# Attention with a top-32 mask and a gated layer: from one slot at a time to pairs of slots, with scores, two sets of values and scores side by side

## The chip, the cores and the metric

The kernel runs on one core of a Trainium2 chip. The metric is the device time of one execution in microseconds. The core has a matmul engine (TensorE, PE in the profile), a vector engine (VectorE, DVE), an engine for functions of one element (ScalarE, ACT), a general one (GpSimd, POOL) and a queue that issues all DMAs here (SyncE, SP). Each takes its own instructions in the order in which the program lists them; semaphores order them among each other.

## The reference

Eight batches, eight heads, 576 positions, 64 elements per head; all in float32.

```python
scores = scale * np.matmul(q, k.transpose(0, 1, 3, 2))       # scale = 1/8
kth = np.partition(scores, -32, axis=-1)[..., -32:-31]
scores = np.where(scores >= kth, scores, -1000000000.0)
scores = scores - np.max(scores, axis=-1, keepdims=True)
attn = np.exp(scores)
attn = attn / (np.sum(attn, axis=-1, keepdims=True) + 1e-09)
attn_out = np.matmul(attn, v)
x = attn_out.transpose(0, 2, 1, 3).reshape(4608, 512)
h = x @ w_in                                                 # 512 -> 2048
out = (h * (1.0 / (1.0 + np.exp(-1.702 * h)))) @ w_out       # 2048 -> 512
```

## The kernel before, in words

**Slots.** The work on attention is cut into 144 slots, 18 per batch. A full slot is one tile of 128 query rows of two heads (four row tiles by four head pairs, 16 slots). The 64 rows that are left over (576 is 4.5 x 128) make two ends slots per batch, each with four heads. In an even batch the ends slots come last, in an odd batch first, so that four ends slots stand together: slots 16 to 19, 52 to 55, 88 to 91, 124 to 127.

**Steps of a slot.**
- `prepare` (L185): TensorE transposes a loaded q or k of two heads in four 128x128 blocks into one PSUM bank; ScalarE copies it to `q_t` or `k_t` (L195). With a k, the 64 leftover rows of q and k are transposed too (L199), into a second bank, and copied out (L200, L202).
- `scores` (L215): matmuls over 64 rows, with the two heads on the two halves of the array (shape 64*128, at ends slots 64*64), into `s_ps`, two tiles of two banks each. ScalarE copies them to `sc` (L232), which has three buffers.
- `topk` (L234): on VectorE, eight largest at a time for each head (L241), then their removal (L244); 14 operations. `two_slots` calls it within `find`.
- `bounds` (L255), two small operations on GpSimd, and `exponentials` (L263), four operations on ScalarE with their sums, writing `pr`.
- `divide` (L276): VectorE takes the reciprocal of the sums; from slot 9 on ScalarE scales the first head's half of `pr` (L288) and GpSimd the second's (L289).
- `turn_main` and `turn_ends` (L312, L316): TensorE transposes `pr` into `tp`; ScalarE copies it to `pt` (L310).
- `values` (L322): TensorE multiplies `pt` with v. The two heads use the two column halves (shape 128*64). ScalarE copies to `xT` (L344, L349).
- `hidden` (L364): 512 hidden units for a tile of 128 tokens, 32 matmul instructions into the only bank of `ph`. `tanh` (L385) has ScalarE make the tanh of it and a copy `h`, and `gate` (L397) multiplies them on GpSimd (in the first ten slots and at the end on VectorE, straight from `ph`). `project` (L411) adds the result's share of the output in `po`, eight matmul instructions. A token tile takes four rounds of these; there is one round per slot.

**PSUM.** `s_ps` takes four banks, `ph` one, `po` one. The other two are the ring `tp`, from which `prepare`, `turn` and `values` take a bank in turn.

**Weights.** The two weight matrices come in 32 pieces during the first nine slots (two to four per slot, `by_slot`). `round_piece` (L122) takes each through five steps: `size` (ScalarE), `shift` (VectorE, L143), `low` and `sign` (ScalarE), `finish` (two GpSimd operations, L138 and L139, in the following slot). The shifts stand between the operations of `topk`, after the seventh.

**Order.** The order of instructions is written out by hand: `slot(n)` lists them. It begins with the loads that the table `later` holds for this slot, then bounds and exponentials of slot n-1, preparations and scores of slot n+2 (up to slot 6), sizes, tanh, the top-k of slot n with the division of n-1 after its sixth operation, and the gate. From slot 7 on ("settled") come preparations, projection, turning and values of n-1, the scores of n+2 and the hidden round:

```python
        if settled and n + 2 < N:
            scores(n + 2)
        hidden()
```

Three tables give the slot, counted from the first slot of a batch, in which a head pair's q and k are loaded (`FETCH`) and prepared (`READY`), and its v loaded (`VALUES`).

Of the kernel before, what the change touches and what calls it, by code (L numbers as in the profile page):

```python
# [9 lines left out]
ALU = mybir.AluOpType  # L10
ENG = mybir.EngineType
F32 = mybir.dt.float32
U32 = mybir.dt.uint32
# [3 lines left out]
P = 128  # L17
# [11 lines left out]
def kernel(  # L29
# [24 lines left out]
    nc = tc.nc  # L54
# [11 lines left out]
    G = 4  # L66
    NG = FC // G
    PIECE = 512
# [8 lines left out]
    SETTLED = 9  # L77
# [3 lines left out]
    const = ctx.enter_context(tc.tile_pool(name="const", bufs=1))  # L81
# [20 lines left out]

    ident = const.tile([P, P], F32, name="ident")
    make_identity(nc, ident[:])
    win = const.tile([P, CC, DFF], F32, name="win")
    wout = const.tile([P, FC, C], F32, name="wout")

# [14 lines left out]
    def round_piece(n):  # L122

        c, g = pieces[n]
        dst = wout[:, g, :] if c is None else win[:, c, g * PIECE : (g + 1) * PIECE]
        words = raw.pop(n)[:].rearrange("p (n w) -> p n w", w=2)
        low, high = words[:, :, 0], words[:, :, 1].bitcast(F32)
        bits, whole = dst.bitcast(U32), dst.bitcast(I32)

        def finish():
            nc.gpsimd.tensor_tensor(out=whole, in0=whole, in1=low.bitcast(I32), op=ALU.add)  # L138
            nc.gpsimd.tensor_tensor(out=dst, in0=dst, in1=high, op=ALU.mult)  # L139

        return {
            "size": lambda: nc.scalar.activation(dst, high, AF.Abs, scale=REBASE),
            "shift": lambda: nc.vector.tensor_scalar(bits, bits, 3, None, op0=ALU.logical_shift_left),  # L143
            "sign": lambda: nc.scalar.activation(high, high, AF.Sign),
            "low": lambda: nc.scalar.mul(out=low.bitcast(I32), in_=low, mul=2.0**-29),
            "finish": finish,
        }
# [37 lines left out]
    def prepare(name, b, hp):  # L185
        src = loaded.pop((name, b, hp))


        before = 0 if name == "q" else TAIL
        dst = qkt.tile([P, S + before], F32, name=f"{name}_t")  # L190
        full = ps_t.tile([P, 512], F32, name="tp")
        for t in range(NF):
            nc.tensor.transpose(full[:, t * P : (t + 1) * P], src[:, t, :, :], ident[:])  # L193
        scale = SCALE if name == "q" else 1.0
        nc.scalar.mul(out=dst[:, before : before + FULL], in_=full[:], mul=scale)  # L195
        (qT if name == "q" else kT)[b, hp] = dst
        if name == "k":
            ends = ps_t.tile([P, 512], F32, name="tp")
            nc.tensor.transpose(ends[:, 0:P], loaded.pop(("ends", b, hp))[:], ident[:])  # L199
            nc.scalar.mul(out=qT[b, hp][:, FULL:S], in_=ends[:, 0:TAIL], mul=SCALE)  # L200
            for to in (0, before + FULL):
                nc.scalar.copy(out=dst[:, to : to + TAIL], in_=ends[:, TAIL:P])  # L202
# [8 lines left out]
    N = len(slots)  # L211
    PER = N // B
    st = [{} for _ in slots]

    def scores(n):  # L215
        b, t, hps = slots[n]
        ps = [ps_s.tile([P, 2, 512], F32, name="s_ps") for _ in range(2)]
        if t < NF:
            parts = [(i, 0, slice(0, P), slice(t * P, (t + 1) * P)) for i in range(2)]
        else:  # L220
            parts = [(i, p, slice(p * TAIL, (p + 1) * TAIL), slice(FULL, S)) for i, p in ((0, 0), (1, 1), (0, 1), (1, 0))]
        for c in range(2):
            for i, p, rows, cols in parts:
                on = slice(i * D, (i + 1) * D)
                nc.tensor.matmul(  # L225
                    ps[i][rows, c, 0:HALF],
                    lhsT=qT[b, hps[p]][on, cols],
                    rhs=kT[b, hps[p]][on, FIRST[i] + c * HALF : FIRST[i] + (c + 1) * HALF],
                )
        sc = st[n]["sc"] = scp.tile([P, 2, S], F32, name="sc")  # L230
        for i in range(2):
            nc.scalar.copy(out=sc[:, i, :].rearrange("p (c k) -> p c k", c=2), in_=ps[i][:, :, 0:HALF])  # L232
# [22 lines left out]
    def bounds(n):  # L255

        top = st[n]["top"]
        cut = st[n]["cut"] = small.tile([P, 2], F32, name="cut")
        low = st[n]["low"] = small.tile([P, 2], F32, name="low")
        nc.gpsimd.tensor_scalar(cut[:], top[:, :, TOPK - 1], -1.0, None, op0=ALU.mult)  # L260
        nc.gpsimd.tensor_tensor(out=low[:], in0=top[:, :, TOPK - 1], in1=top[:, :, 0], op=ALU.subtract)
# [50 lines left out]
    def turn_main(n):  # L312
        for i in range(2):
            turn(n, i * NF, MAIN[i], NF)

    def turn_ends(n):  # L316

        turn(n, 2 * NF, FULL, 1)
# [42 lines left out]
    to_gate, gated, to_project = [], [], []  # L361
    proj = {}

    def hidden():  # L364
        if not ready:
            return
        xT, rows = ready[0]
        g = hidden_at["g"]
        ph = ps_h.tile([P, G, P], F32, name="ph")
        for i in range(G):  # L370
            f = g * G + i
            for c in range(CC):
                nc.tensor.matmul(  # L373
                    ph[:, i, :],
                    lhsT=win[:, c, f * P : (f + 1) * P],
                    rhs=xT[:, c, :],
                    start=(c == 0),
                    stop=(c == CC - 1),
                )
        to_gate.append((ph, g, rows))  # L380
        hidden_at["g"] = (g + 1) % NG
        if g == NG - 1:
            ready.pop(0)
# [47 lines left out]
    later = {}  # L431
# [4 lines left out]

    READY = (((-9, -8), (-7, -6), (-5, -4), (-3, -2)), ((-7, -6), (-5, -4), (-3, -3), (-2, -2)))
    FETCH = (((-13, -12), (-11, -10), (-7, -6), (-5, -4)), ((-11, -10), (-9, -8), (-6, -5), (-4, -3)))  # L440
    VALUES = ((-8, -7, -1, 0), (-8, -7, 0, 0))
    by_slot = dict(enumerate([2, 3, 4, 4, 4, 4, 3, 4, 4]))
    for n in by_slot:
        first = sum(map(len, list(by_slot.values())[:n]))
# [19 lines left out]
    def slot(n):  # L464
        todo = later.pop(n, [])
        for fn, args in todo:
            if fn is not prepare:
                fn(*args)
        preparing = [args for fn, args in todo if fn is prepare]
        settled = n > PROJECTS  # L470
        aside = SETTLED < n < N
        before = 0 <= n - 1 < N
        if before:
            bounds(n - 1)
            exponentials(n - 1)
        if n < 0:
            for m in range(2):
                for args in preparing:
                    if args[2] == m:
                        prepare(*args)  # L480
                scores(m)
        elif not settled:
            for args in preparing:
                prepare(*args)
            scores(n + 2)
        some = [round_piece(x) for x in by_slot.get(n, [])]
        for piece in some:
            piece["size"]()
        shifts = [piece["shift"] for piece in some]
        tanh(aside)  # L490
        for i, op in enumerate(topk(n) if 0 <= n < N else [lambda: None] * 14):
            op()
            if i == 2 and unfinished:
                unfinished.pop(0)()
            if i == 5:
                if before:
                    divide(n - 1)
                while unfinished:
                    unfinished.pop(0)()
            if i == 11 and not aside:  # L500
                gate(aside)
            if i > 6 and shifts:
                shifts.pop(0)()
        if aside:
            gate(aside)
        if settled:
            for args in preparing:
                prepare(*args)
        for piece in some[:2]:
            piece["low"]()  # L510
        going = settled and len(to_project) > (2 if n < N else 0)
        if going:
            project(range(G - 1))
        if before:
            turn_main(n - 1)
        if going:
            project(range(G - 1, G))
        if before:
            turn_ends(n - 1)
        for piece in some[2:]:  # L520
            piece["low"]()
        if before:
            values(n - 1)
        for piece in some:
            piece["sign"]()
            unfinished.append(piece["finish"])
        if settled and n + 2 < N:
            scores(n + 2)
        hidden()

    with tc.manual_schedule():
        for n in range(-1, N + 1):
            slot(n)
        n = N + 1
        while ready or to_gate or gated or to_project:
            slot(n)
            n += 1
# [30 lines left out]
```

## Time and profile before

| | |
|---|---|
| median of 3 runs | 1668.62 us (1666.99 to 1668.85) |
| span of the profiled execution | 1667.9 us |
| busy: PE, DVE, ACT, POOL | 96%, 88%, 69%, 45% |
| slots 0 to 8 (with weight steps), start to start on DVE | 19.0 us, then 13.6 to 14.9 us |
| settled full slots without preparation | 10.60 us |
| settled full slots with a q, with a k | 11.04, 11.15 us |
| slots 16, 17, 52, 53, 88, 89, 124, 125 | 13.43 us six times, 13.71 and 15.13 us |
| last top-k operation to the end | 47 us |

A slot is read on VectorE from its first L241 on `sc` to the next slot's. In the chain of waits each line gives a start, a length and the work that the end depended on at that time; lengths there are from start to the next start, so that they add up. A matmul's modelled duration in the timeline is longer than its step, since matmuls overlap. A float32 matmul of two operand tiles appears as two instructions. The shape after MATMUL (128*128, 64*128, 128*64) gives the rows and columns of the array that one instruction uses.

### The profile page before, as it was taken

How to read it: one execution, taken by the hardware profiler on the slowest of the kernel's cores; microseconds unless marked ns; L12 is line 12 of the kernel's file. 1: busy time of each engine (PE TensorE's matmuls, PEld its weight loads, DVE VectorE, ACT ScalarE, POOL GpSimd, SP SyncE). 2: the span in 40 equal slices, each digit the busy share in tenths (PEclk: the TensorE clock that was granted, in tenths of full speed). 3: DMA queues.
4: the chain of work that ended last, by engine and by line, in shares of the span. 5: the costliest groups of instructions: out<-in, count | busy, mean ns of one | idle time of the engine just before them, and what ended most of it. 6: DMA issues, size and time to landing. Idle time of an engine off the chain costs nothing.

```text
span 1667.9 us, 31998 instructions
## 1 busy us (share of the span) xinstructions
PE 1599.2 (96%) x11923; PEld 1174.2 (70%) x11923; DVE 1468.8 (88%) x3210; ACT 1155.7 (69%) x2450; POOL 753.0 (45%) x785
## 2 busy tenths in 40 slices
PE   5579999999999999999999999999999999999999
PEld 3466767777777767777777776777777776777776
DVE  4999989998999988998899997999899998899980
ACT  5987766677766676667776676667777676777661
POOL 1787434444444443444444443444444444444440
PEclk7789999999999999999999999999999999999999
DMA  7342100110001100111001110011000110000000
GB/s 211 115 151 62 23 23 14 36 36 22 21 8 42 29 22 22 36 28 30 22 7 28 29 36 16 8 36 36 22 21 8 43 29 22 22 7 8 7 8 13
DMA packets 125723, 56.59 MB, mean 34 GB/s; under 512 B 116864, under 2 KB 116864, under 8 KB 125568
## 3 DMA queue, kind: packets, MB, share of 16 engines
q1 hardware_dynamic: 125568, 54.55, 12.4%
q8 instruction: 94, 1.54, 0.4%
q14 instruction: 61, 0.50, 0.1%
HBM read 45.09 MB, written 9.44 MB: 33 GB/s over the span
## 4 chain that ended last, share of the span: by engine, by line
PE 87%; DVE 5%; ACT 5%; SPq 1%; issue 1%; POOL 1%; DMA 0%; POOLq 0%; ACTq 0%
PE ph L373 29%; PE po L421 29%; PE o L332 10%; PE s_ps L225 10%; PE tp L300 8%; DVE top L241 2%; DVE left L244 2%; ACT pr L271 1%; PE tp L193 1%; ACT sc L232 1%; DVE wout L143 1%; ACT sc L269 1%; ACT pr L288 0%; SPq L160 0%; DVE win L143 0%
## 5 line engine op out<-in xcount | busy, mean ns | idle before, releaser
L241 DVE MAX8 top<-left 128x8 f32<-128x576 f32 x864 | 610.0, 746 | 0.0
L289 POOL TENSOR_SCALAR pr<-pr,rden 128x576 f32<-128x576 f32 x135 | 232.9, 1725 | 688.8 <-ACT th L390 640.7
L421 PE MATMUL po<-wout,gT 128*128 128x512 f32 x1152 | 542.4, 594 | 0.0
L373 PEld LDWEIGHTS ph<-xT,win 128*128 128x128 f32 x4096 | 470.6, 193 | 56.0 <-issue 47.6
L373 PE MATMUL ph<-xT,win 128*128 128x128 f32 x4096 | 494.4, 279 | 6.4 <-DVE gT L406 6.4
L244 DVE MATCH_REPLACE8 left<-top,left 128x576 f32<-128x576 f32 x576 | 423.3, 742 | 0.0
L310 ACT COPY pt<-tp 128x512 f32<-128x512 f32 (+1 forms) x432 | 193.4, 481 | 192.0 <-PE tp L300 185.6
L421 PEld LDWEIGHTS po<-wout,gT 128*128 128x128 f32 x1152 | 198.3, 192 | 142.6 <-issue 142.4
L232 ACT COPY sc<-s_ps 128x576 f32<-128x576 f32 x288 | 169.9, 642 | 134.8 <-PE s_ps L225 134.6
L271 ACT ACTIVATE pr<-sc,low 128x576 f32<-128x576 f32 x288 | 219.5, 767 | 0.0
L300 PEld LDWEIGHTS tp<-ident,pr 128*128 128x128 f32 x1215 | 145.0, 140 | 104.7 <-issue 42.3
L269 ACT ACTIVATE sc<-sc,cut 128x576 f32<-128x576 f32 x288 | 208.7, 779 | 9.2 <-POOL cut L260 9.2
L244 DVE MATCH_REPLACE8 left<-top,sc 128x576 f32<-128x576 f32 x288 | 211.6, 742 | 0.0
L241 DVE MAX8 top<-sc 128x8 f32<-128x576 f32 x288 | 201.9, 742 | 10.7 <-ACT sc L232 10.7
L403 POOL TENSOR_SCALAR th<-th 128x512 f32<-128x512 f32 x134 | 200.6, 1497 | 0.0
L225 PE MATMUL s_ps<-k_t,q_t 64*128 64x288 f32 (+1 forms) x1280 | 182.2, 431 | 1.3 <-ACT k_t L195 1.3
L300 PE MATMUL tp<-ident,pr 128*128 128x128 f32 x1215 | 177.2, 273 | 0.3 <-POOL pr L289 0.2
L404 POOL TENSOR_TENSOR gT<-th,h 128x512 f32<-128x512 f32 x134 | 171.5, 1280 | 11.2
L332 PEld LDWEIGHTS o<-pt,v_l 128*64 128x64 f32 x2560 | 128.0, 138 | 67.8 <-ACT pt L310 67.8
L332 PE MATMUL o<-pt,v_l 128*64 128x128 f32 (+1 forms) x2560 | 161.7, 269 | 0.2
L280 DVE TENSOR_SCALAR some<-den 128x2 f32<-128x2 f32 x144 | 24.1, 168 | 130.6 <-ACT pr L271 130.4
L225 PEld LDWEIGHTS s_ps<-k_t,q_t 64*128 64x128 f32 (+1 forms) x1280 | 99.6, 177 | 40.2 <-issue 20.9
(50 smaller groups left out, 1152.3 us busy)
## 6 DMA issues: line engine op xcount, KB each, us to landing
q_l<-in_q_dram SPq DMA_DIRECT2D x64, 128.0 KB, 2.5
k_l<-in_k_dram SPq DMA_DIRECT2D x64, 128.0 KB, 2.6
v_l<-in_v_dram SPq DMA_DIRECT2D x64, 128.0 KB, 2.5
raw<-in_moe_w_in_dram SPq DMA_DIRECT2D x16, 512.0 KB, 4.3
raw<-in_moe_w_out_dram SPq DMA_DIRECT2D x16, 512.0 KB, 3.7
out_dram<-ob SPq DMA_DIRECT2D x32, 256.0 KB, 2.1
ends<-in_q_dram SPq DMA_DIRECT2D x32, 32.0 KB, 2.3
ends<-in_k_dram SPq DMA_DIRECT2D x32, 32.0 KB, 2.4
```

The costliest lines, as they stand in the source:

```text
L225: nc.tensor.matmul(ps[i][rows, c, 0:HALF], lhsT=qT[b, hps[p]][on, cols], rhs=kT[b, hps[p]][on, FIRST[i] + c * HALF : FIRST[i] + (c + 1) * ...
L241: nc.vector.max(top[:, i, 8 * r : 8 * r + 8], (left if r else sc)[:, i, :])
L244: nc.vector.match_replace(left[:, i, :], top[:, i, 8 * r : 8 * r + 8], (left if r else sc)[:, i, :], LOWEST)
L269: nc.scalar.activation(sc[:, i, :], sc[:, i, :], AF.Prelu, bias=cut[:, i : i + 1], alpha=HUGE)
L271: nc.scalar.activation(pr[:, i * S : (i + 1) * S], sc[:, i, :], AF.Exp, bias=low[:, i : i + 1], accum_out=den[:, i : i + 1],)
L289: nc.gpsimd.tensor_scalar(pr[:, S : 2 * S], pr[:, S : 2 * S], rden[:, 1:2], None, op0=ALU.mult)
L300: nc.tensor.transpose(tp[:, c * P : (c + 1) * P], pr[:, at], ident[:])
L310: nc.scalar.copy(out=to, in_=tp[:, 0 : blocks * P])
L332: nc.tensor.matmul(o[j * D : (j + 1) * D, 0 : cols.stop - cols.start], lhsT=main[:, c, j, :] if c < NF else tail[:, j, :], rhs=pt[:, j * N ...
L373: nc.tensor.matmul(ph[:, i, :], lhsT=win[:, c, f * P : (f + 1) * P], rhs=xT[:, c, :], start=(c == 0), stop=(c == CC - 1),)
L403: nc.gpsimd.tensor_scalar(th[:], th[:], 1.0, None, op0=ALU.add)
L421: nc.tensor.matmul(po[:], lhsT=gT[:, i, :], rhs=wout[:, f, :], start=(f == 0), stop=(f == FC - 1))
```

## The change

Five things change.

1. From slot 10 on, `two_slots(n)` replaces two calls of `slot`. It softens n-1 (bounds and exponentials), finds the top-k of n, turns n-2, makes a hidden round, softens n, turns n-1, finds the top-k of n+1, and then has the scores of n+2, the values of n-2 and n-1, and the scores of n+3 in a row, with a second hidden round last. Values come one slot later relative to the rest than before. Up to four preparations have places: after the first gate, after the second gate, before the scores, and after the last scores.
2. `READY`, `FETCH` and `VALUES` have new entries for the later head pairs of a batch.
3. A piece's `shift` is a `scalar_tensor_tensor` with a second input, a column of zeros that is broadcast, in place of a `tensor_scalar`.
4. In the first slots all `size` steps come ahead of preparations and scores, and the gate on VectorE comes after the ninth operation of `topk` rather than the twelfth.
5. In settled slots that are still single, only the first preparation stays in its place; others come after the scores.

```diff
+    none = const.tile([P, 1], U32, name="none")
+    nc.vector.memset(none[:], 0)
...
-            "shift": lambda: nc.vector.tensor_scalar(bits, bits, 3, None, op0=ALU.logical_shift_left),
+            "shift": lambda: nc.vector.scalar_tensor_tensor(
+                out=bits, in0=bits, scalar=3, in1=none[:].to_broadcast([P, PIECE]),
+                op0=ALU.logical_shift_left, op1=ALU.bitwise_or,
+            ),
...
-    READY = (((-9, -8), (-7, -6), (-5, -4), (-3, -2)), ((-7, -6), (-5, -4), (-3, -3), (-2, -2)))
-    FETCH = (((-13, -12), (-11, -10), (-7, -6), (-5, -4)), ((-11, -10), (-9, -8), (-6, -5), (-4, -3)))
-    VALUES = ((-8, -7, -1, 0), (-8, -7, 0, 0))
+    READY = (((-9, -8), (-7, -6), (-4, -3), (-2, -1)), ((-7, -6), (-4, -3), (-3, -2), (-1, -2)))
+    FETCH = (((-13, -12), (-11, -10), (-7, -7), (-5, -4)), ((-11, -10), (-9, -8), (-5, -5), (-2, -2)))
+    VALUES = ((-8, -7, 0, 0), (-8, -7, 2, 2))
...
-        elif not settled:
+        some = [round_piece(x) for x in by_slot.get(n, [])]
+        for piece in some:
+            piece["size"]()
+        if 0 <= n and not settled:
             for args in preparing:
                 prepare(*args)
             scores(n + 2)
-        some = [round_piece(x) for x in by_slot.get(n, [])]
-        for piece in some:
-            piece["size"]()
...
-            if i == 11 and not aside:
+            if i == 8 and not aside:
                 gate(aside)
...
         if settled:
-            for args in preparing:
+            for args in preparing[:1]:
                 prepare(*args)
...
         if settled and n + 2 < N:
             scores(n + 2)
+        if settled:
+            for args in preparing[1:]:
+                prepare(*args)
         hidden()
 
+    def two_slots(n):
...
+        preparing = [get(first)[:1], get(second)[:1], get(first)[1:], get(second)[1:]]
...
+        def find(m):
+            for i, op in enumerate(topk(m) if live(m) else [lambda: None] * 14):
+                op()
+                if i == 5 and live(m - 1):
+                    divide(m - 1)
+
+        def middle(m):
+            go = going()
+            if go:
+                project(range(G - 1))
+            if live(m) and "pr" in st[m]:
+                turn_main(m)
+            if go:
+                project(range(G - 1, G))
+            if live(m) and "pr" in st[m]:
+                turn_ends(m)
+
+        begin(first)
+        soften(n - 1)
+        tanh(aside)
+        find(n)
+        gate(aside)
+        prepare_some()
+        middle(n - 2)
+        hidden()
+        begin(second)
+        soften(n)
+        tanh(aside)
+        gate(aside)
+        prepare_some()
+        middle(n - 1)
+        find(n + 1)
+        prepare_some()
+        for m in (n + 2, n - 2, n - 1, n + 3):
+            if m > n and live(m):
+                scores(m)
+            elif m < n and live(m) and "pt" in st[m]:
+                values(m)
+        prepare_some()
+        hidden()
+
     with tc.manual_schedule():
-        for n in range(-1, N + 1):
+        for n in range(-1, SETTLED + 1):
             slot(n)
-        n = N + 1
+        for n in range(SETTLED + 1, N + 1, 2):
+            two_slots(n)
+        n += 2
         while ready or to_gate or gated or to_project:
             slot(n)
             n += 1
```

More of the change, by code (lines that the diff above doesn't have):

```diff
@@ L528, in slot, with begin, prepare_some, soften @@
             scores(n + 2)
+        if settled:
[3 more added lines that the diff above has]
+    def two_slots(n):
+        first, second = [later.pop(m, []) for m in (n, n + 1)]
+        get = lambda todo: [args for fn, args in todo if fn is prepare]
+        preparing = [get(first)[:1], get(second)[:1], get(first)[1:], get(second)[1:]]
+        def begin(todo):
+            for fn, args in todo:
+                if fn is not prepare:
+                    fn(*args)
+        def prepare_some():
+            for args in preparing.pop(0):
+                prepare(*args)
+        live = lambda m: 0 <= m < N
+        going = lambda: len(to_project) > (2 if n < N else 0)
+        aside = n < N
+        def soften(m):
+            if live(m):
+                bounds(m)
+                exponentials(m)
+        def find(m):
[35 more added lines that the diff above has]
+        prepare_some()
         hidden()
     with tc.manual_schedule():
-        for n in range(-1, N + 1):
+        for n in range(-1, SETTLED + 1):
             slot(n)
-        n = N + 1
+        for n in range(SETTLED + 1, N + 1, 2):
+            two_slots(n)
+        n += 2
         while ready or to_gate or gated or to_project:
```

## The prediction

> **What bounds the kernel now.** I read the page, then the chain of waits stage by stage (0 to 140 us, 160 to 1620, the tail), then the timeline of single slots.
>
> ```profile
> PE 1599.2 (96%) x11923; PEld 1174.2 (70%) x11923; DVE 1468.8 (88%) x3210; ACT 1155.7 (69%) x2450; POOL 753.0 (45%) x785
> PE 87%; DVE 5%; ACT 5%; SPq 1%; issue 1%; POOL 1%; DMA 0%; POOLq 0%; ACTq 0%
> ```
>
> TensorE carries 87% of the chain that ended last. VectorE has 88% busy time, so it stands close behind. From 160 us on, the chain is TensorE alone, slot after slot. One slot (800 to 850 us; start, length, what):
>
> ```profile
> 831.33 2.58 PE po L421 x6
> 833.91 0.88 PE tp L300 x8
> 834.78 0.86 PE po L421 x2
> 835.64 0.11 PE tp L300
> 835.75 1.24 PE o L332 x20
> 836.99 1.17 PE s_ps L225 x8
> 838.16 3.77 PE ph L373 x32
> ```
>
> The sum is 10.60 us. The same work costs less where the previous work has the same shape. In the tail, with no values or scores ahead of it, the hidden layer reads:
>
> ```profile
> 1633.08 3.44 PE po L421 x8
> 1636.51 3.57 PE ph L373 x32
> ```
>
> So 0.20 of the 3.77 us is the step from 64*128 (scores) back to 128*128. In the same way, 20 value matmuls are ten side-by-side pairs at 0.11 us (8 transposes of equal width take 0.87), 1.09 us; the row has 1.24: 0.15 for the step to 128*64. Score pairs start 0.24 us apart in the timeline (826.67, 826.91, 827.15), four are 0.97, the row has 1.17: 0.20 for that step. Each slot pays 0.55 us for three steps.
>
> The second loss is at the ends slots. Eight slots (16 and 17 of each 36) last 13.43 to 15.13 us. They prepare a q and its k together:
>
> ```profile
> 223.11 1.18 ACT sc L232 x2
> 224.29 0.72 ACT sc L269 x2
> ...
> 225.52 1.62 ACT pr L271 x4
> 227.14 0.45 ACT th L390
> ...
> 227.98 0.79 ACT pr L288
> 228.77 0.50 ACT q_t L195
> ...
> 229.31 0.33 PE tp L199
> ```
>
> The two-buffer ring of transposes is full with q and k. The ends transpose waits until ScalarE, in order behind scores, exponentials, tanh and scaling, copies q out.
>
> The third place is the stage with weight steps, before 142 us. There VectorE carries most of the chain, with 13.6 to 14.9 us a slot, and hardly waits from slot 3 on:
>
> ```profile
> 25.86 0.41 DVE L143 TENSOR_SCALAR win<-win 128x512 uint32<-128x512 uint32 x1
> 26.19 0.75 DVE L241 MAX8 top<-left 128x8 f32<-128x576 f32 x1
> ...
> 119.26 1.30 POOL L138 TENSOR_TENSOR wout<-wout,raw 128x512 int32<-128x512 int32 x1
> 119.30 1.55 DVE L143 TENSOR_SCALAR wout<-wout 128x512 uint32<-128x512 uint32 x1
> 120.77 0.75 DVE L241 MAX8 top<-left 128x8 f32<-128x576 f32 x1
> ```
>
> Alone, a shift takes 0.33 us to the next start. Beside a running GpSimd operation it takes 1.47 for the first of a slot and 0.71 to 0.78 for the others.
>
> **What the Trainium skill says.** "TensorEngine Tiling (Array Packing)", Key Properties: changing the tiling mode, not merely the tile, drains TensorE. The trace agrees: 0.15 to 0.20 us at each of the three changes, nothing between tiles of one mode. "SBUF — State Buffer", Who interferes with whom: a VectorE operation in a two-port mode and a GpSimd operation block each other entirely, and so do a VectorE operation with two SBUF inputs and a GpSimd operation that reads SBUF. The trace agrees on the first half (1.47 against 0.33); no row of before shows the second, and it is what prices the new shift.
>
> **The change part by part.** Sums against the profiled span of 1667.9; the three runs have a median of 1668.62, 0.7 higher.
>
> (a) Pairs. Two slots of before have six changes of shape, 2 x 0.55 = 1.10 us. A pair goes 128 rows, scores, both values, scores, 128 rows: 0.20 + 0.15 + 0.20 + 0.20 = 0.75. The step from scores to values, and the one from full width to scores, aren't in the trace; their bounds are 0 and twice the nearest row, and I take 0.15 and 0.20, as for the neighbours. 66 pairs with scores x 0.35 = -23 us; bounds -46 and 0. The matmuls themselves stay.
>
> Whether TensorE keeps the pair at 2 x 10.60 - 0.35 = 20.85 is a matter of waits. I count from TensorE's start of a pair's first project: transposes 2.6 to 3.4, hidden 4.4 to 8.0, second transposes 10.6 to 11.5, ends transpose 12.3, scores from 12.4, values from 13.6, scores 15.9 to 17.1, hidden to 20.85. VectorE needs per slot 8 maxima and 6 removals in twins of 1.32 and 1.46 us and 0.35 for the division: 10.0, so 20.0 a pair. The tightest loop starts at the end E of find(n). Bounds and exponentials take 3.2 (end of find 1620.57, tanh 1623.78), tanh and h copy 0.9, the first pt copy 0.65: the ends transpose can start at E + 4.8. Then 0.11 + 1.17 + 1.24 + 1.09 + 1.17 to the end of the second scores; score copies 1.1, exponentials 2.9, division 0.4, eight more operations 5.6: the end of find(n+2) is E + 19.6. That is 1.25 us under TensorE's 20.85, so TensorE stays the bound; VectorE idles 0.85 a pair at the division, less than the 1 us a slot of now. On ScalarE, the second sc copy, both o copies and the softening of n+1 wait behind each other, inside this loop. On GpSimd, the scaling of n comes behind the second gate (1.50 + 1.28), about 15 us into the pair, and is used 8 us later. The one bank of ph is read by about 1.5 and 10.7, written from 4.4 and 17.1: no wait.
>
> (b) q and k apart. Eight slots cost 10.60 + 0.99 for q, k and ends when nothing waits; they took 13.43 six times, 13.71 and 15.13 (TensorE ran slow for 1.6 us there): 6 x 1.84 + 2.12 + 3.54 = 16.7. In the pair (16, 17) the order is k, then q after the gate, then k before the scores; each copy leaves before the ring comes round, with 0.2 us to spare at the tightest. I take -16; bounds -17 and +3. The loads of each q or k (two DMAs and one for ends) move with it on SP. The latest, q and k at -2 for use in the same pair, need six issues of 0.6 and 2.6 to land, 6.2 us, and TensorE asks after 8. Values of odd b at +2 come a whole pair ahead of their use. Nothing but loads stands behind them on SP.
>
> (c) The shift. Two inputs and no two-port mode: 0.60 by the nearest row (gate L406, same width, next start 0.60 later) against 0.33. If it still has to wait for GpSimd, each of the 27 shifts of slots 2 to 8 lengthens by 0.22 to 0.27, all on the chain: +6. If it doesn't, they take 0.60 in place of 0.91 on average: -8, of which ScalarE, some 12.6 us of steps in those slots of 13.7, leaves -5. By the skill I take +6.
>
> (d) Size first. In slot 0 VectorE waits 8.55 us for a size that stands behind a late k and its scores. Size first removes this wait. But exponentials and signs of slots 0 and 1 still follow the loads of q, k, and I get 29.3 for the division of slot 0 (33.7 before), and about 1.7 us earlier for that of slot 1: -2; bounds -6 and 0. The score copies that size moves ahead of are used two slots later. The gate three operations earlier costs VectorE the same, its tanh is done by then: 0. The memset stands ahead of the first scores: 0.
>
> (e) Hand-over and two-tile ends. Values(10) and (11) come a pair later, so the second pair has one hidden group less and TensorE may idle some 3 us; the first pair gains about as much. Values of two ends slots use four o tiles in a ring of two: +0.3 for each of four boundaries. +1 in all; bounds -3 and +5.
>
> Sum: -23 - 16 + 6 - 2 + 1 = -34; 1667.9 - 34 + 0.7 = 1634.6, said as **1634**.
>
> **The rivals.**
> 1. As summed, 1634: 0.55.
> 2. The new shift doesn't wait for GpSimd: 11 less, 1623. For it: 1.47 us is plainly the two-port form's. Against: the skill's second half. 0.2.
> 3. Half the gain: the change straight from 64 rows to 64 columns costs as much as is saved (1657), or a ring or late load keeps the ends stalls (1651). 0.17.
> 4. Slower: the loop through ScalarE becomes the bound. Its place is the pt copy of the second slot, now behind the softening of n. It decides from 20.85 + 34/66, about 21.4 us, 1.8 over my sum. At 22.0, for instance if bounds wait for GpSimd's gate and score copies fall behind the scaling, it's 66 x 1.15 = +76: 1710. Against: ScalarE has only 14.5 us of steps in a pair. 0.08.
>
> **How the numbers follow.** About 0.2%, 3.3 us, is what a measurement of this kernel can tell from no change. Case 1 with its bounds reaches from 1624 to 1646. Case 2 with a larger gain from the changes of shape goes to 1612, case 3 to 1657; leaving out the slower case and the outermost of the others gives 1612 to 1656. Faster 0.90 (cases 1 to 3, save a sliver), same 0.03, slower 0.07.
>
> **What would show it.** In the chain of settled pairs: scores 1.17, values together 2.3, scores 1.17, hidden alternating 3.57 and 3.77, a pair of 20.85. No slot pair near 26.9 at the ends. The shift row near 1.1 us mean (rival 2: 0.65). Division waits under 1 us a pair. I'm wrong if ends transposes wait for pt copies, if a pair without preparations is over 21.2, or if values behind scores take over 2.5.

## The result and the profile after

The changed kernel takes 1643.43 us (median of 4 runs, 1643.06 to 1644.08) against 1668.45 (4 runs): ratio 0.9852, 95% interval 0.9835 to 0.9869. It is 25 us faster. The forecast was 1634 with a range of 1612 to 1656; 9 of the 34 us that it summed did not come. The changed kernel's lines stand five further down from the top part on (L300 is L305, L373 is L378, L421 is L426; L143 is L145).

The page of the changed kernel: busy time by engine, then the chain that ended last.

```profile
PE 1578.7 (96%) x11923; PEld 1179.0 (72%) x11923; DVE 1497.8 (91%) x3212; ACT 1155.6 (70%) x2449; POOL 756.2 (46%) x783
PE 88%; DVE 8%; ACT 2%; POOL 1%; issue 1%; DMA 0%; SPq 0%; POOLq 0%; ACTq 0%
```

The same number of matmul instructions takes 20 us less, so TensorE's work itself became cheaper. VectorE has 29 us more busy time and a larger share of the chain; that is mostly the shifts of the first stage and a wait inside one of its small operations, both below.

**Settled pairs.** The chain of waits of the changed kernel (start, length, what) at the end of a pair:

```profile
1553.94 3.57 PE ph L378 x32
...
1561.94 1.17 PE s_ps L230 x8
1563.11 2.33 PE o L337 x40
1565.44 1.17 PE s_ps L230 x8
1566.61 3.77 PE ph L378 x32
```

Two sets of values take 2.33, not 2 x 1.24, and one of the two hidden rounds has lost its 0.20. A pair without preparations lasts 20.86 us on VectorE (10.61 + 10.25), where two slots lasted 21.20.

**The ends slots.** The chain at the boundary between two batches, with one q or k at a time:

```profile
620.36 0.44 PE tp L198 x4
...
625.22 0.44 PE tp L198 x4
625.66 0.25 PE tp L204
625.91 1.13 PE s_ps L230 x16
```

No ScalarE step stands between a preparation and the next matmul. The pairs (16, 17) and (18, 19), which hold the four ends slots, last 22.27 and 22.35 us: 20.86 and little more than their transposes.

**The first stage.** The chain in slot 6 of the changed kernel:

```profile
106.27 1.80 DVE wout L145
108.07 0.67 DVE top L246
108.74 0.59 DVE gT L411
109.33 1.69 DVE wout L145
111.02 0.67 DVE top L246
111.69 1.03 DVE wout L145
```

The first shift takes 1.80 in place of the 1.47 us that the prediction read in the kernel before, the third 1.03 in place of 0.77. The second, which now has the gate ahead of it, takes 1.69.

**The hand-over.** TensorE's timeline where single slots end and pairs begin (start, length, what, idle time before and who ended it):

```profile
188.38 1.35 PE L305 MATMUL tp<-ident,pr 128*128 128x128 f32 x9
193.74 0.47 PE L305 MATMUL tp<-ident,pr 128*128 128x128 f32 x1 [4.01 <-ACT pt L315]
194.14 2.29 PE L230 MATMUL s_ps<-k_t,q_t 64*128 64x288 f32 x8
196.36 1.97 PE L337 MATMUL o<-pt,v_l 128*64 128x128 f32 x16
```

In pair (12, 13) no token tile is ready for the first hidden round. TensorE reaches the ends transpose of slot 11 early, waits 4.0 us for a copy, and then runs the next scores and values at about half speed: the profile gives a granted clock of 0.53 for 194.0 to 200.5 us and of 1.00 right after.

Starts of slots on VectorE, from each kernel's timeline, in us:

| kernel | slot 3 | slot 10 | from 3 to 10 | slot 10 to the end of the span |
|---|---|---|---|---|
| before | 57.1 | 152.5 | 95.4 | 1515.4 |
| changed | 55.1 | 157.5 | 102.4 | 1484.8 |
| changed, old shift | 54.7 | 151.0 | 96.2 | 1486.2 |
| changed, gate back | 56.4 | 156.5 | 100.1 | 1484.8 |
| changed, other order in pair (12, 13) | 55.5 | 157.8 | 102.3 | 1482.5 |
| before, new shift | 59.3 | 160.9 | 101.5 | 1515.8 |
| before, size first | 54.5 | 148.5 | 94.0 | 1513.7 |

### The profile page after: what moved, and what is told of

The parts are those of the page before. It is cut to its first block, busy times and chain, and to the rows that moved or that the text cites. A ratio compares the mean times of both kernels' runs of the same rounds, so it can differ in the third digit from the quotient of the medians.

```text
span 1642.3 us, 31956 instructions
## 1 busy us (share of the span) xinstructions
PE 1578.7 (96%) x11923; PEld 1179.0 (72%) x11923; DVE 1497.8 (91%) x3212; ACT 1155.6 (70%) x2449; POOL 756.2 (46%) x783
## 4 chain that ended last, share of the span: by engine, by line
PE 88%; DVE 8%; ACT 2%; POOL 1%; issue 1%; DMA 0%; SPq 0%; POOLq 0%; ACTq 0%
PE ph L378 30%; PE po L426 29%; PE s_ps L230 10%; PE o L337 9%; PE tp L305 8%; DVE top L246 3%; DVE left L249 2%; PE tp L198 2%; DVE wout L145 1%; DVE win L145 1%; ACT sc L237 1%; DMA k_l<-in_k_dram 0%; ACT pr L276 0%; PE tp L204 0%; POOL wout L141 0%
## 5 line engine op out<-in xcount | busy, mean ns | idle before, releaser
L426 PE MATMUL po<-wout,gT 128*128 128x512 f32 x1152 | 541.3, 593 | 0.0
L378 PEld LDWEIGHTS ph<-xT,win 128*128 128x128 f32 x4096 | 468.1, 192 | 41.8 <-issue 41.0
L378 PE MATMUL ph<-xT,win 128*128 128x128 f32 x4096 | 485.1, 277 | 0.0
L426 PEld LDWEIGHTS po<-wout,gT 128*128 128x128 f32 x1152 | 197.6, 191 | 142.0 <-issue 141.8
L305 PEld LDWEIGHTS tp<-ident,pr 128*128 128x128 f32 x1215 | 145.5, 141 | 108.7 <-issue 59.3
L305 PE MATMUL tp<-ident,pr 128*128 128x128 f32 x1215 | 177.2, 273 | 5.0 <-ACT pt L315 4.0
L337 PEld LDWEIGHTS o<-pt,v_l 128*64 128x64 f32 x2560 | 133.5, 139 | 31.6 <-ACT pt L315 16.1
L265 POOL TENSOR_SCALAR cut<-top 128x2 f32<-128x2 f32 x144 | 32.2, 224 | 221.4 <-DVE top L246 217.3
```

Source lines behind the costliest of these rows:

```text
L305: nc.tensor.transpose(tp[:, c * P : (c + 1) * P], pr[:, at], ident[:])
L337: nc.tensor.matmul(o[j * D : (j + 1) * D, 0 : cols.stop - cols.start], lhsT=main[:, c, j, :] if c < NF else tail[:, j, :], rhs=pt[:, j * N ...
L378: nc.tensor.matmul(ph[:, i, :], lhsT=win[:, c, f * P : (f + 1) * P], rhs=xT[:, c, :], start=(c == 0), stop=(c == CC - 1),)
L426: nc.tensor.matmul(po[:], lhsT=gT[:, i, :], rhs=wout[:, f, :], start=(f == 0), stop=(f == FC - 1))
```

## Experiments

The theory after the result: the pairs gain what was forecast (two changes of shape, and the ends slots), the first stage loses 5 us because the new shift still waits for GpSimd, and the hand-over loses 8 to 9. The main rival: the gain is one of spread waits, and the shift is innocent.

**Old shift in the changed kernel.**

```diff
-            "shift": lambda: nc.vector.scalar_tensor_tensor(
-                out=bits, in0=bits, scalar=3, in1=none[:].to_broadcast([P, PIECE]),
-                op0=ALU.logical_shift_left, op1=ALU.bitwise_or,
-            ),
+            "shift": lambda: nc.vector.tensor_scalar(bits, bits, 3, None, op0=ALU.logical_shift_left),
```

> The changed kernel with its old shift (tensor_scalar). Theory: the two-input shift waits for GpSimd like the old one and holds the port longer, so it cost some 7 us between slots 2 and 10; with the old shift slot 10 starts about 150.5 us in place of 157.5, and as TensorE only becomes continuous after that, the whole goes to about 1636. Rival: the 13 us that the first stage lost between slots 1 and 10 are those of size first and of the earlier gate; then the old shift changes nothing, 1643.

Measured: 1637.66 us, ratio to before 0.9816 (0.9800 to 0.9833), 5.8 under the changed kernel. From slot 3 to slot 10 it is 6.1 faster (102.37 against 96.23 before rounding). Slot 6 in its chain:

```profile
102.70 1.54 DVE wout L143
104.24 0.67 DVE top L241
104.91 0.58 DVE gT L406
105.49 1.43 DVE wout L143
106.92 0.67 DVE top L241
107.59 0.77 DVE wout L143
```

Each contended shift is 0.26 us shorter in the old form. The second one, behind the gate, is at 1.43 here too, against 0.77 in the kernel before: that part is not the shift's.

**New shift in the kernel before.** The opposite edit, alone.

> The kernel before with the two-input shift alone. Theory: a contended shift goes from 1.47 to 1.7 us (first of a slot) and from 0.71-0.78 to 1.0 (others), slot 10 starts some 7 us later, 1668.5 becomes about 1675. Rival: the new shift is neutral or frees VectorE: 1660 to 1668.

Measured: 1678.16 us, ratio 1.0060 (1.0045 to 1.0075), slower by more than the 7 us expected. From slot 3 to slot 10 it loses 6.1 us, the same as in the changed kernel; another 2.2 are lost before slot 3, which the changed kernel doesn't show (55.1 against 54.7 with the old shift). From slot 3 on, the shift's cost doesn't depend on the pairs.

**No finish.** The changed kernel without the two GpSimd operations per piece:

```diff
         def finish():
-            nc.gpsimd.tensor_tensor(out=whole, in0=whole, in1=low.bitcast(I32), op=ALU.add)
-            nc.gpsimd.tensor_tensor(out=dst, in0=dst, in1=high, op=ALU.mult)
+            pass
```

> The changed kernel without the two GpSimd operations that finish a weight piece (they are left out, so the weights are not the reference's). Theory: the shifts wait for these operations; without them each new shift takes 0.6 us to the next start, slots 2 to 8 about 12.5 us (10.0 + 4 x 0.6, or what ScalarE allows, 12.6), and slot 10 starts at about 140. Rival: the new shift is slow by itself, 1.0 us and more with GpSimd idle.

Measured: 1624.76 us (one run), slot 10 at 140.6. VectorE's timeline there:

```profile
87.79 0.67 DVE L144 SCALAR_TENSOR_TENSOR win<-win,none 128x512 uint32<-128x512 uint32 x1
88.38 0.08 DVE L248 MATCH_VALUE_LOAD left<-top,left 128x8 f32 x1
```

Without these GpSimd operations the new shift takes 0.59 us to the next start. So it's the wait for them that makes 1.03 to 1.80 of it.

**Size first in the kernel before.**

> The kernel before with all sizes ahead of preparations and scores, nothing else. Theory: VectorE's 8.55 us wait in slot 0 goes, but exponentials of slots 0 and 1 stay behind the loads of q and k, so slot 1 starts 8 us earlier, slot 3 only 2 us: about 1666. Rival: the whole wait is gained: 1660.

Measured: 1664.28 us, ratio 0.9976 (0.9967 to 0.9986). Slot 1 starts 8.0 us earlier, slot 3 only 2.6, as in the theory; 1.4 more come in slot 6, which I hadn't foreseen (a shift waits 1.6 us for its size there in the kernel before, and no longer does), and 4.0 stay at slot 10. The time lies between the theory's 1666 and the rival's 1660.

**Gate back to its place.** `if i == 11` again in the changed kernel.

> The changed kernel with the gate of the first slots back behind the twelfth operation. Theory: behind the ninth it falls between the first and the second shift, the second shift then misses its turn and waits for a whole GpSimd operation (1.69 in place of 1.04 us), four slots, 2.6 us: about 1640.8, slot 10 at about 155. Rival: the earlier gate frees TensorE's hidden bank and is neutral or a gain: 1643 or more.

Measured: 1642.82 us, ratio 0.9841 (0.9827 to 0.9856). From slot 3 to slot 10 it gains 2.3 us, close to the 2.6 expected. But its slot 3 started 1.3 later than the changed kernel's (three kernels with the same first stage, the changed one and the two with six changes of shape below, start slot 3 at 55.1, 55.9 and 56.2), so the median shows 0.6, which the intervals don't separate from nothing. On top of the old shift and the other order in pair (12, 13), the same edit is clear of noise: 2.8 us (1636.16 to 1633.35, under "All three back"). The timelines show the mechanism, first in the changed kernel, then with the gate back:

```profile
109.19 1.28 POOL L140 TENSOR_TENSOR win<-win,raw 128x512 int32<-128x512 int32 x1
109.25 1.76 DVE L145 SCALAR_TENSOR_TENSOR wout<-wout,none 128x512 uint32<-128x512 uint32 x1
```

```profile
109.25 1.10 DVE L145 SCALAR_TENSOR_TENSOR wout<-wout,none 128x512 uint32<-128x512 uint32 x1
109.77 1.74 POOL L140 TENSOR_TENSOR win<-win,raw 128x512 int32<-128x512 int32 x1
```

Behind the gate, the second shift starts just after GpSimd has begun its next operation. Without the gate ahead of it, it comes before that operation.

**Second preparation after the scores, alone.** The kernel before with `preparing[:1]` in place and `preparing[1:]` behind the scores.

> The kernel before, in which the second preparation of a settled slot comes after the scores (as in the change's single slots). Theory: the ends slots lose 13.43 - 11.59 = 1.84 us each because q and k together fill the ring; apart, those eight slots go to 11.6 and the time falls by 16.7 to about 1652. Rival: the time lies in the ends slots' own scores and not in the preparation: nothing changes, 1668.

Measured: 1653.50 us, ratio 0.9912 (0.9898 to 0.9927): 14.7 less by the medians. Slots 16 and 17 read 11.83 and 11.49 us in place of 13.43 each, and the other three couples the same within 0.01. In its chain the preparation stands behind the scores without a ScalarE step:

```profile
218.32 1.13 PE s_ps L225 x16
219.46 0.59 PE tp L193 x4
220.04 0.11 PE tp L199
220.15 3.57 PE ph L373 x32
```

**Six changes of shape, first try.** The changed kernel with the last piece of the pair's second projection between its two values:

```diff
+            if m == n - 2 and go:
+                project(range(G - 1, G))
```

> The changed kernel with the last two matmuls of the pair's second projection moved between its two values, so that a pair changes the array's shape six times again and not four. Theory: two changes of shape cost 0.20 + 0.15 us, 66 pairs, +23: about 1666, pair 21.2 us. Rival: the pair is faster because waits are spread better over two slots, and the changes of shape are hidden: 1643 to 1648.

Measured: 1696.47 us, ratio 1.0170 (1.0155 to 1.0186). That is 53 more and not 23; neither expectation. The chain shows what came with it:

```profile
815.90 0.45 PE tp L305 x4
...
816.37 0.59 ACT pt L315
...
817.01 0.33 PE tp L305
```

With nothing between the transposes, the ends transpose runs into the copy of the first bank. Pairs without preparations last 21.66 us in place of 20.86, so with 0.35 for the shapes this wait is worth 0.45 a pair: 66 x (0.35 + 0.45) = 53.

**Six changes of shape without this wait.** A third piece of the projection stays between the transposes.

```diff
-                project(range(G - 1))
+                project(range(G - 1 - later_piece))
...
-            if go and not later_piece:
-                project(range(G - 1, G))
+            if go:
+                project(range(G - 1 - later_piece, G - later_piece))
```

> The six changes of shape again, without the wait of the first try: a third of the projection's first part moves between the second slot's transposes, so that the ends transpose no longer runs into its pt copy, and the last third goes between the two values. Theory: only the two changes of shape are left, 0.35 us a pair, 1643.4 + 23 = about 1666, and the pair of 21.2 us shows 1.24 for each set of values. Rival: the first try's 53 us were all waits; then 1643 to 1650.

Measured: 1679.28 us, ratio 1.0059 (1.0042 to 1.0076), 36 more than the changed kernel. The chain of a pair without preparations:

```profile
878.57 1.17 PE s_ps L230 x8
879.74 1.24 PE o L337 x20
880.98 1.05 PE po L426 x2
882.03 1.24 PE o L337 x20
883.28 1.17 PE s_ps L230 x8
884.45 3.77 PE ph L378 x32
```

Such pairs last 21.20 us, 0.35 over 20.86: 2.48 for two values in place of 2.33, and 1.05 for two projection matmuls in place of 0.86. That is 23 of the 36. Most of the other 13 lie in pairs that prepare a q or a k: some of them last 22.43 us in place of 21.30 or 22.81 in place of 21.84. TensorE's waits between 210 and 1600 us (us in total, times, longest):

```profile
PE tp L305 <- ACT q_t L200: 4.2, 10, 0.6
PE tp L305 <- ACT k_t L200: 4.0, 10, 0.4
```

The changed kernel has no wait in this list. At such a place the chain leaves TensorE:

```profile
806.82 0.82 ACT sc L274 x2
...
808.17 1.61 ACT pr L276 x4
809.78 0.48 ACT th L395
810.26 0.47 ACT h L398
810.73 0.50 ACT k_t L200
...
811.28 1.09 PE tp L305 x8
```

This is the loop of the prediction (find, softening, tanh, copies, scores, next softening). Here k's copy (0.50) stands in it, ahead of the transposes, and this edit adds the two projection matmuls between the values (1.05) and the second step to the shape of the values (0.15). From one end of find to the next it takes 22.81 us here, which is the length of this pair; in the changed kernel the pair lasts 21.84. Without the 1.05 and the 0.15 the loop would be about 21.6 by this estimate, 0.2 under the pair. So in pairs with preparations its margin is small.

**Turning slot 11 before softening slot 12.**

```diff
+        if n == SETTLED + 3:
+            middle(n - 1)
         soften(n)
...
-        middle(n - 1)
+        if n != SETTLED + 3:
+            middle(n - 1)
```

> The changed kernel with the second half of pair (12, 13) in another order: TensorE turns slot 11 before slot 12 is softened. Theory: at the hand-over the pair has no hidden round and TensorE stands 4.0 us at the ends transpose behind a pt copy that ScalarE makes only after softening 12, and then runs at half clock for 2.9 us of work; without this wait about 1638. Rival: VectorE's first pairs are the bound there, and the wait comes back in the next pair: 1643.

Measured: 1642.52 us, ratio 0.9846 (0.9829 to 0.9863). The 4.0 us wait is gone, and another stands a little later:

```profile
196.05 1.88 PE L230 MATMUL s_ps<-k_t,q_t 64*128 64x288 f32 x8 [2.12 <-ACT sc L237]
197.86 5.32 PE L378 MATMUL ph<-xT,win 128*128 128x128 f32 x32
```

TensorE is slow there again (5.3 for a hidden round). After slot 10 this order is 2.3 us shorter than the changed kernel, not 5; the medians differ by 0.9, and the ranges of the two overlap. The rival is mostly right: the wait came back, later in the same pair. That TensorE, with one hidden round less to do, must wait for VectorE at one place or another fits this, but only this one other order was run.

**Old shift and this order.**

> Both: old shift and the other order in pair (12, 13). If the two losses add up: 1643.4 - 7 - 5 = about 1631. If the hand-over only takes what the first stage gave: 1636.

Measured: 1636.16 us, ratio 0.9806 (0.9791 to 0.9821); 7.3 under the changed kernel, about the sum of the measured 5.8 and 0.9. The number is that of the second case, but the two gains add up; what was too large were the 7 and the 5 put in.

**All three back.** Old shift, gate after the twelfth operation, other order in pair (12, 13).

> Old shift, gate back at its place, and the other order in pair (12, 13). If the three add up: 1643.4 - 5.8 - 2.6 - 0.9 = about 1634, faster than both kernels. If what the first stage gains is lost at the hand-over: 1636 as without the gate.

Measured: 1633.35 us (1632.83 to 1634.08), ratio to before 0.9786 (0.9772 to 0.9801). The intervals of this and of the changed kernel (0.9835 to 0.9869) don't meet: it is faster than the changed kernel too, by about 10 us. The expected 1634 was right.

**Shifts in a row.** The former, with `while i == 7 and shifts` in place of one shift per operation.

> The former with all shifts of a slot in a row after the eighth operation. If a waiting GpSimd operation doesn't come in between, a slot pays one wait and four times 0.33: 2.4 in place of 3.7 us, six slots, about 1634 - 8 = 1626. If GpSimd comes in between after each shift, every shift waits 1.4: 5.6 us a slot, +12: 1646.

Measured: 1646.71 us, ratio 0.9865 (0.9851 to 0.9880), 13 slower than the former: the second case. Slot 6 in its chain:

```profile
110.42 4.33 DVE wout L143 x3
114.75 1.32 DVE top L241 x2
```

Three shifts take 3 x 1.44. In the timeline of this slot GpSimd's next operation comes in after each, so bundling the waits gained nothing here.

The new tables of loads and preparations (part 2 of the change) and the order in the single settled slots of the changed kernel (part 5) were not run apart from the pairs.

## Why the prediction was right, and where it was off

(a) **Pairs**: -23 forecast. Scores 1.17, values 2.33, a pair at 20.86 where the sum said 20.85 and two slots took 21.20: 66 x 0.345 = -23. The experiment without the extra wait put 0.35 us back for two changes of shape. The step from scores straight to values, which the trace of before didn't show, costs what the neighbours do (0.15 of the 2.33). Rival 3's first half falls.

(b) **q and k apart**: -16 forecast. The eight waits of TensorE behind the copy of q (1.67 us each, one of 1.95) are gone, so about all of the 16.7 is gained; the one-part experiment got 14.7 of it in the kernel before. Rival 3's second half falls.

(c) **The shift**: +6 forecast, +6.1 measured between slots 3 and 10, in both kernels. The Trainium skill's statement on two SBUF inputs ("SBUF — State Buffer", Who interferes with whom), which no row of before could show, holds here: 0.59 alone, 1.03 to 1.80 beside GpSimd. Rival 2 falls. The row's mean is 1.23 and 1.37 us for the two matrices, not "near 1.1"; with the gate back in its place it is 1.19 and 1.27.

(d) **Size first and the gate**: -2 forecast for size, -4.0 measured at slot 10 in the kernel before. The step that failed is "The gate three operations earlier costs VectorE the same, its tanh is done by then: 0". It costs 2.3 us between slots 3 and 10, and 2.8 in the whole time on top of the other two edits. I had priced the operation and its wait, not what it does to the next: it moves the second shift by 0.6 us, past the end of one GpSimd operation and into the next. The sum of (c) and (d), +4, came out as +5 by luck: an error of 2 in size and one of 2.3 in the gate cancel.

(e) **The hand-over**: the term that was mis-sized. "TensorE may idle some 3 us; the first pair gains about as much", +1 in all, up to +5. Measured after slot 10: 1484.8 - 1515.4 = -30.6 against -23 - 16.7, so +9, where the sum had +1. Of it 4.0 is the idle time, foreseen as some 3; 2.9 the slow scores and values after it (2.22 + 4.13 against 1.17 + 2.33 in the chain); 1.0 a wait for a q copy in pair (10, 11). The step that failed is "the first pair gains about as much": no such gain shows after slot 10, and the slow matmuls after the idle time weren't in the sum. The wait of 4.0 us is also the one listed wait of an ends transpose for a pt copy from slot 10 on, which the prediction named as a sign of being wrong. About 1 us is left, and the batch boundaries lose about as much: the four sets of ends values at a boundary take 2 x 1.32 + 1.65 + 1.32 us of TensorE's timeline in the kernel before and 2.80 + 2.77 in the changed one. That is nearly the same, though each of the two pairs should save 0.15 there; the second set waits for ScalarE's copy of the first out of the two-buffer ring. So "+0.3 for each of four boundaries" was right.

(f) **Rival 4**, the loop through ScalarE, is not the bound in the changed kernel: the profile lists no wait of TensorE from 205 to 1600 us, and the chain leaves it only at the batch boundaries, for the copies just named. With 1.2 us more in the loop and a k to copy it is the bound in some pairs (22.81 against 21.84). VectorE's waits at the division came to 73.7 us in 66 waits, 1.1 each, where the sum had 0.85 and the sign was "under 1 us". The margin of 1.25 us for a pair without preparations was not measured by itself.

Sum: +5 - 23 - 17 + 9 = -26; the spans differ by 25.6. The 9 was read as what was left after slot 10; its parts, 4.0, 2.9, 1.0 and about 1, were read by themselves.

One reading of the kernel before was too short: its chain is not "TensorE alone" from 160 us on. It leaves TensorE at the ends slots, as the prediction says further down, and from 1600.7 to 1617.0 us, ahead of the tail.

## What to carry to other kernels

Where TensorE is the bound, read the chain for the same group of matmuls behind different neighbours: the difference is the price of a change of shape, and putting groups of one shape together pays it fewer times. Check the ring and the copy that the new order leans on; moving one small group of matmuls cost more by the wait that it uncovered than by its shapes. When a pipeline gets a slot longer, price its start on its own: here the engine that had no slack to lose lacked a round of work, and slow matmuls followed. And run each part of a change alone: here the new shift and the earlier gate cost time, and the gain of the other parts hid it.

## What the runs showed of the hardware that I had not expected

- A VectorE operation of two columns waits too. The first division step (`some`, 128x2) has a mean of 168 ns in the kernel before and 316 in the changed one, where one of the two of a pair now falls beside GpSimd's gate (0.49 us at 837.13, with the gate from 836.99; 0.17 at 848.07, with GpSimd idle). That is why the second half of a pair has 10.25 us on VectorE and not 10.0. From the changed kernel's groups by shape (count, busy us, mean ns, idle before):

```profile
L285 DVE TENSOR_SCALAR some<-den 128x2 f32<-128x2 f32 x144 | 45.6, 316 | 81.3 <-ACT pr L276 81.3
```

- After a wait of 4.0 us in the changed kernel, of 2.1 with the other order in pair (12, 13), and of 1.95 at 623.4 us in the kernel before, TensorE ran the following 4 to 7 us at about half to three quarters of its speed: 4.13 us for two sets of values in place of 2.33, 5.32 for a hidden round in place of 3.84, 4.26 for six projection matmuls in place of 2.58. After the other seven waits at the ends slots of the kernel before, of 1.66 to 1.67 us, it did not: the six projection matmuls took 2.58 all seven times.
- In the slot shown, a waiting GpSimd operation came in between shifts that stood one behind the other: 1.44 us each in place of 0.33.
